# A transformer layer with shared keys and values: two accumulators for the row sums of P, ten P slots, a layer norm split between VectorE and GpSimd, and a new set of planner constants

## The chip, the cores and the metric

The kernel runs on one core of one Trainium2 chip. The core has five engines that run their own instruction streams: TensorE (PE in the profile; its weight loads are listed apart as PEld), VectorE (DVE), ScalarE (ACT), GpSimd (POOL) and SyncE (SP), which here only issues DMAs. The engines wait for one another with semaphores. Data lies in HBM, in the on-chip memory SBUF (128 partitions), and in PSUM, where TensorE writes its results. The metric is the time of one execution on the device in microseconds. Of several executions the median counts.

## What is computed

One layer with 2048 tokens of width 1024: attention with 32 heads of width 32, which all share one key and one value head, then a gated feed-forward of width 3584. All inputs are bf16.

```python
h  = x + attention(layernorm(x)) @ wo
h2 = h + (sigmoid(g) * u) @ w_down      # g = layernorm(h) @ w_gate, u = layernorm(h) @ w_up

# attention, for each of 32 heads
scores = q @ k.T * 32 ** -0.5           # k and v are the same for all heads
p = softmax(scores)
o = p @ v
```

The layer norm subtracts the mean and divides by sqrt(variance + eps).

## The kernel before

**One list for each engine.** The kernel doesn't write its instructions in program order. A planner (class `Plan`) keeps a list for each engine and a model clock. The main loop walks along TensorE's time: it asks which piece of work is ready, appends it to TensorE's list, and the work of the other engines that depends on it goes into heaps, from which `step` takes the one that can start first (of those, the lowest `prio`, which is the most urgent). Every operation carries two costs: `occ`, how long its engine is taken, and `lat`, until its result can be used. Times in the model are ns. At the end the lists are emitted, with semaphore waits where one engine needs another's result. So a changed constant in the dictionary `TUNE` changes the order of instructions on every engine, though not what each computes.

**Halves.** The 16 token tiles of 128 tokens are worked on one after another, and each in two halves of 16 heads: `hf` runs from 0 to 31, `c = hf // 2` is the tile. A half has 16 rounds, one for each key tile `kt`. A round is called S: four matmuls with 32 rows each, on the four row groups of TensorE at once, which write scores of 128 keys by 2048 (head, token) columns into four PSUM banks. Two exponentials on ScalarE (L696), 1024 columns each, write them as bf16 into a **P slot** (`Pr`, 4 KB a partition). PSUM has three pairs of banks for this (`S_ps`), and two banks (`F_ps`) for everything else. The first two halves are interleaved, and four more areas of SBUF serve as slots (`extra`) until their real users come.

**Sums and PV.** The softmax needs the sum of P over all keys. VectorE adds the slots of a half into one accumulator, `acc` (L671): slot 0 plus slot 1, then each further slot, 15 additions. After the last one, TensorE sums over the partitions with 32 small matmuls on `acc` (class SUM). VectorE takes the reciprocal (L737), and two DMAs (L739 and L740) spread it over the partitions. Since there is one accumulator, the first addition of half `hf` waits for SUM of `hf - 1`; if that isn't planned yet, additions are kept in `late_adds` and made up by `flush_adds`. Half 0 is in `RAW`: its sums come from matmuls with a matrix of ones instead. PV multiplies P by V in parts of some rounds (`parts_of`: two parts of eight from half 2 on), in column mode: four matmuls on four column groups. A slot is free when its PV matmuls and its addition are done. A PV part may be chosen only when all its additions are planned, and when `in_row` says so: TensorE is in row mode (just after S), or, with `col_ok`, in column mode, or no more than a given number of slots is free (`pv_few` for PV, `sum_few` for SUM).

**After a tile's two halves**: VectorE multiplies by the reciprocal (`OT`, L754), TensorE multiplies by wo (class OP), VectorE adds x, and the second layer norm follows (`stats` with `ph` 1): statistics on VectorE (L344 to L355), then on GpSimd variance plus eps (L367), power one half (L370) and power minus one (L373), then the normalization on VectorE (L866, tile `hn`) and a transposing DMA to `hnT`. The first layer norm (`ph` 0) runs at the start over x; its first two tiles already use one GpSimd power between two VectorE operations (L359 to L365).

**Feed-forward.** Class GU makes gate and up products in pieces of 512 of the 3584 columns, seven groups of two pieces; ScalarE takes a tanh (L978), VectorE multiplies (L999 or L985). Usually `hnT` is the stationary operand, the result has tokens on partitions, and a transposing DMA (L1008) turns it. For the first `ws0` and the last `ws1` tiles the weights are stationary (`held_w`), which needs no transpose and takes four times as many matmuls of a quarter of the columns. Class D makes the down product in four quarters. Gate and up weights are streamed from HBM for every tile (`load_next`), two units at a time, into eight units of a ring; after the last S, the P slots become such units too.

**Order.** TensorE takes S as soon as its inputs are known and ScalarE has less than 700 ns of work queued; otherwise it goes on with the group in hand, or picks a new one from the classes in the order of `PRIOS`. `start_of` keeps VectorE's additions (`prio` 6) out of a window `hold` around the expected end of TensorE's group, so that VectorE is free to empty its bank. `evac` gives copies out of PSUM to ScalarE or VectorE, whichever is free first, with a bias (`eb` for x, K and V, `eq` for Q) against ScalarE.

Of the kernel before, what the change touches and what calls it, by code (L numbers as in the profile page):

```python
# [15 lines left out]
SEM = 75.0  # L16


TUNE = dict(warm=70, late=400, ws0=1, ws1=2, parts0=3, parts1=4, lord=2, h_ord=0, ho=3, ho2=0, pvl1=0, pvl2=1,
            col_ok=1, pace0=310, swait=400, parts=2, raw=1, rl=0, nd=4, pc=16, rate=315, pace=280, xd=4, qf=1,  # L20
            dall=0, wo_late=1, nkn=2, few=1, rmin=900, hmin=1, h0=0, h1=600, hf=1.35, run=700, sum_few=2,
            pv_few=4, d_off=1, d_a=-1, d_b=-1, eb=150, eq=1000)


class Op:
# [16 lines left out]
class Plan:  # L42
# [53 lines left out]
    def start_of(self, o):  # L96

        s = max(self.free[o.eng], o.ready)
        if o.eng == "dve" and o.prio >= 6 and s < self.hold[1] and s + o.occ > self.hold[0]:
            return self.hold[1]  # L100
        return s

    def step(self, limit):
# [21 lines left out]
        if o.nbytes:  # L125
            if o.pace:
                self.pace_free = s + o.nbytes / TUNE["pace0" if self.fast(s) else "pace"]
            k = o.key.rstrip("0123456789_")
            go = max(s + 1720.0, self.dma_free)
            w = self.SLOW.get(k, 1.0) if k != "ha" else 2.5 if o.nbytes < 200000 else 1.3  # L130
            self.dma_free = go + o.nbytes * w / TUNE["rate"]
            o.end = self.dma_free + 700.0 + self.LATE.get(k, 0.0) + TUNE["late"]
        else:
# [24 lines left out]
def t_dve(n, rate=0.96, fix=158.0):  # L158
    return dict(occ=n / rate + fix - 90.0, lat=n / rate + fix + SEM)
# [5 lines left out]
def bass_sequential_preLN__grouped_kv_mqa__glu_gated_glu__prompt_kernel(  # L165
# [24 lines left out]
    NSLAB = 4  # L190
    SW = 512
    NGR = NFT // 4
    NP = 11
    xf = A_x[0]
    of = out[0]

    with ExitStack() as es:
        def EC(cm):
            return es.enter_context(cm)

        def SB(name, shape, dt=BF16):
            return EC(nc.sbuf_tensor(name, [P] + shape, dt))
# [2 lines left out]
        zone = SB("zone", [NFT * D])  # L205
        ring_t = SB("ring", [NSLAB * DT * SW])
        Pr = SB("Pr", [NP, 2048])
        acc = SB("acc", [2048])
        QTb = SB("QTb", [2, NG, 256])
        wo_sb = SB("wo_sb", [NG, D])  # L210
        kT4 = SB("kT4", [S])
# [98 lines left out]

        for c in ["xxqxxqxxxxxxqxxxxq", "qxqxxqxqxxxxxxxxxx", "xqxqxqqxxxxxxxxxxx", "xqxqxqxqxxxxxxxxxx", "xxqxqxqxqxxxxxxxxx"][TUNE["lord"]]:
            if c == "x":
# [19 lines left out]
        def stats(ph, tiles, srcs, deps, prio, after=((), ())):  # L332
            t0, k = tiles[0], len(tiles)

            def slow(n, wait):

                n += wait if ph and t0 < NT - 1 else 0
                return dict(occ=n, lat=n + 100)

            ag = []  # L340
            for t, src, dp in zip(tiles, srcs, deps):
                s = n_st[0] % 8
                n_st[0] += 1
                a = pl.op("dve", lambda s=s, src=src: DVE.bn_stats(st[:, s, 0, :], src[:, 0:512]), dp, prio=prio,  # L344
                          occ=600, lat=756, order=[st_user.get(s)] + list(after[0]))
                b = pl.op("dve", lambda s=s, src=src: DVE.bn_stats(st[:, s, 1, :], src[:, 512:1024]), dp, prio=prio,  # L346
                          occ=600, lat=756, order=[st_user.get(s)] + list(after[1]))
                c = pl.op("dve", lambda s=s, t=t: DVE.bn_aggr(mv[:, ph, t, :], st[:, s, :, :]), [a, b], prio=prio - 1,
                          occ=110, lat=284)
                st_user[s] = c  # L350
                ag.append(c)
            tk = slice(t0, t0 + k)
            d = pl.op("dve", lambda: DVE.tensor_copy(out=mvb[:, ph, tk, :], in_=mv[:, ph, tk, :]), ag, prio=prio - 1,  # L353
                      occ=90, lat=250)
            e = pl.op("dve", lambda: DVE.tensor_copy(out=mvr[:, ph, tk, :], in_=mvb[:, ph, tk, :]), [d], prio=prio - 1,  # L355
                      occ=90, lat=250)
            if not ph and t0 < 2:

                f = pl.op("dve", lambda: DVE.tensor_scalar(  # L359
                    out=zb[:, ph, tk], in0=mvb[:, ph, tk, 1], scalar1=LN_EPS_BF16, scalar2=None, op0=ALU.add),  # L360
                    [d], prio=prio - 1, occ=90, lat=250)
                g = pl.op("pool", lambda: POOL.tensor_tensor(
                    out=dsb[:, ph, tk], in0=zb[:, ph, tk], in1=half[:, 0:k], op=ALU.pow), [f, c0], prio=0,
                    **slow(460 + 180 * k, 0))
                h = pl.op("dve", lambda: DVE.reciprocal(rstd[:, ph, tk], dsb[:, ph, tk]), [g], prio=prio - 1, occ=90, lat=250)  # L365
                return e, h
            f = pl.op("pool", lambda: POOL.tensor_scalar(  # L367
                out=zb[:, ph, tk], in0=mvb[:, ph, tk, 1], scalar1=LN_EPS_BF16, scalar2=None, op0=ALU.add),
                [d], prio=prio - 1, **slow(330, 920))
            g = pl.op("pool", lambda: POOL.tensor_tensor(  # L370
                out=dsb[:, ph, tk], in0=zb[:, ph, tk], in1=half[:, 0:k], op=ALU.pow), [f, c0], prio=prio - 1,
                **slow(460 + 180 * k, 900))
            h = pl.op("pool", lambda: POOL.tensor_tensor(  # L373
                out=rstd[:, ph, tk], in0=dsb[:, ph, tk], in1=negone[:, 0:k], op=ALU.pow), [g, c1], prio=prio - 1,
                **slow(400 + 180 * k, 0))
            return e, h
# [5 lines left out]
        def center(t):  # L382
            if t >= TUNE["pc"]:
                xcent[t] = pl.op("pool", lambda t=t: POOL.tensor_scalar(
# [30 lines left out]
        for tiles in ([0], [1], [2, 3], [4, 5], [6, 7], [8, 9], [10, 11], [12, 13], [14, 15]):  # L415
            after = ((), ())
            if tiles[0] in (1, 2):

                p = tiles[0] - 1
# [218 lines left out]
        sum_last = {}  # L638
# [14 lines left out]
        RAW = tuple(range(TUNE["raw"])) + ((NH - 1,) if TUNE["rl"] else ())  # L653
        rs_b = h_sb[:, 2, :].bitcast(F32)

        def make_add(hf, kt):

            pred = hf - 1
            if pred not in RAW and pred not in sum_last:
                late_adds[hf].append(kt)  # L660
                return
            a = acc[:, :]
            slot = slot_of[(hf, kt)]
            dp = [exp_of[(hf, kt, i)] for i in range(2)]
            if kt == 1:
                in0 = slot_of[(hf, 0)]
                dp += [exp_of[(hf, 0, i)] for i in range(2)] + [sum_last.get(pred)]
            else:
                in0 = a
                dp.append(add_op[(hf, kt - 1)])  # L670
            add_op[(hf, kt)] = pl.op("dve", lambda: DVE.tensor_tensor(out=a, in0=in0, in1=slot, op=ALU.add), dp, prio=6,  # L671
                                     **t_dve(2048, 1.92))

        def flush_adds(hf):
            for kt in late_adds.pop(hf, []):
                make_add(hf, kt)
# [42 lines left out]
        rd_ld = {}  # L719
# [4 lines left out]
            return v_done[0] >= NV or pl.pe_mode == "row" or len(free_slots) <= few or TUNE["col_ok"] and pl.pe_mode == "col"  # L724

        def mk_SUM(hf):
            a = acc[:, :]

            def atoms(b):
                return [(mm(F_ps[DH * j:DH * (j + 1), b, 0:64], sel[:, bb, :], a[:, j * 512 + bb * 64:j * 512 + (bb + 1) * 64],  # L730
                            bb == 0, bb == 7, tile_position=(0, DH * j)), 64, "col" if j == 3 else "col-", [])
                        for bb in range(8) for j in range(4)]

            def after(b, last):
                sum_last[hf] = last
                flush_adds(hf + 1)
                rc = pl.op("dve", lambda: DVE.reciprocal(r_sb[:, :], F_ps[:, b, 0:64]),  # L737
                           [last, rd_ld.get(hf - 1)], prio=0, occ=64 * 8 / 0.96 + 20, lat=64 * 8 / 0.96 + 90 + SEM)
                rd_ld[hf] = dma(lambda: SP.dma_start(r_dram, r_sb[0:P:4, :]), "rd", 8192, [rc] + (rb_ld[hf - 1] if hf - 1 not in RAW else []), prio=0)  # L739
                rb_ld[hf] = [dma(lambda j=j: SP.dma_start(  # L740
                    rb[DH * j:DH * (j + 1), :], bass.AP(r_dram.tensor, r_dram.offset + 512 * j, [[0, DH], [1, 512]])),
                    "rb", 65536, [rd_ld[hf], ot_ev.get(hf - 1), ot_ev.get(0)], prio=0) for j in range(4)]
                finish(hf)
                return [rc]
            return Group("SUM", atoms, lambda: [add_op.get((hf, NT - 1)), c_sel], after, lambda: in_row(TUNE["sum_few"]))
# [341 lines left out]
        while True:  # L1087
# [15 lines left out]
            if v < NV:  # L1103
                run = max(pl.free["act"], t) + sum(o.occ for o in pl.heap["act"])
# [30 lines left out]
            if cur is not None:  # L1135
                at = cur[1][cur_i]
                if known(at[3], t):
                    mode = at[2]
                    o = pe_op(at[0], at[1], "col" if mode == "col-" else mode, at[3] + (cur[2] if cur_i == 0 else []),
                              mode != "col-")  # L1140
# [152 lines left out]
```

## Time and profile before

| What | Value |
|---|---|
| median of 9 executions | 1102.61 us (1099.27 to 1103.95) |
| the profiled execution, its own time | 1100.76 us |
| its span, first to last instruction | 1099.0 us |
| TensorE matmul busy | 1078.4 us (98%), 10686 matmuls |
| ScalarE busy | 1003.5 us (91%) |
| VectorE busy | 834.4 us (76%) |
| GpSimd busy | 65.3 us (6%) |
| exponentials (L696) | 1024 in all, last one ends at 1012.0 us |
| additions into `acc` (L671) | 465, 1.16 to 1.22 us each |
| GpSimd power operations in the second layer norm (L370, L373) | 1.37 and 1.38 us each in 200 to 1000 us |
| granted TensorE clock | 1.00 throughout |
| HBM traffic | 203.82 MB read, 8.12 MB written, 193 GB/s |

Engine times are the union of an engine's instructions. Matmuls, exponentials and additions are pipelined, so the duration of one is longer than the distance from its start to the next; where it is said how often something can be done, the distance between starts is the measure. A matmul group in the profile is told by its tiles: `S_ps<-QTb,kT` is S, `F_ps<-Pr,Vt` is PV, `F_ps<-acc,sel` is SUM, `F_ps<-wo_sb,OT` is OP, `F_ps<-ring,hnT` is GU, with `hnT,ring` or `hnT,Pr` when the weights are stationary, and `F_ps<-zone,hact` is D.

### The profile page before, as it was taken

What the parts mean: (1) busy time and instruction counts of PE and PEld (TensorE: products, weight loads), DVE (VectorE), ACT (ScalarE), POOL (GpSimd) and SP (SyncE); (2) the same over time, 40 slices, a digit from 0 to 9 for tenths busy, and PEclk for the clock granted to TensorE, in tenths of its full rate; (3) what the DMA queues carried; (4) which work ended last, traced back from release to release, by engine and by line L of the source; (5) the groups of instructions that cost most, each with busy time, mean ns of one, the idle gap of its engine ahead of it and who ended that gap; (6) DMA issues with size and microseconds to landing.
All of it is one profiled execution on the core that took longest, in us unless ns stands there. A gap on an engine that the chain in (4) does not pass through costs nothing.

```text
span 1099.0 us, 25839 instructions
## 1 busy us (share of the span) xinstructions
PE 1078.4 (98%) x10686; PEld 542.6 (49%) x10686; DVE 834.4 (76%) x1055; ACT 1003.5 (91%) x1151; POOL 65.3 (6%) x93
## 2 busy tenths in 40 slices
PE   8899999999999999999999999999999999999999
PEld 6433366444444444444444444444444444436898
DVE  8979887778978687878868686888878686887411
ACT  4999999999999999999999999999999999998110
POOL 3300001010100101010000101010000101010000
DMA  8794389967859595876859496876959596786991
GB/s 247 112 310 125 107 258 317 276 181 211 256 164 270 128 275 155 246 201 198 268 154 261 129 275 162 237 219 189 279 134 259 134 257 175 219 224 182 308 315 62
DMA packets 292804, 232.91 MB, mean 212 GB/s; under 512 B 95824, under 2 KB 279120, under 8 KB 292688
## 3 DMA queue, kind: packets, MB, share of 16 engines
q1 hardware_dynamic: 292688, 231.27, 74.6%
q8 instruction: 84, 1.38, 0.5%
q14 instruction: 32, 0.26, 0.1%
HBM read 203.82 MB, written 8.12 MB: 193 GB/s over the span
## 4 chain that ended last, share of the span: by engine, by line
ACT 44%; PE 35%; issue 7%; DVE 7%; DMA 5%; SPq 2%; POOL 0%; DVEq 0%
ACT Pr L696 41%; PE F_ps L440 30%; PE S_ps L440 5%; DVE acc L671 3%; DMA rb<-r_scratch 2%; ACT tnh L978 2%; DMA r_scratch<-r_sb 1%; SPq L740 1%; DMA ring<-in_A_x_dram 1%; DVE st L346 1%; DMA hnT<-hn 1%; DVE st L344 1%; DMA zone<-ring 0%; SPq L298 0%; DVE h_sb L860 0%
## 5 line engine op out<-in xcount | busy, mean ns | idle before, releaser
L696 ACT ACTIVATE Pr<-S_ps 128x1024 bf16<-128x1024 f32 x1008 | 948.3, 1102 | 5.5 <-PE S_ps L440 5.4
L671 DVE TENSOR_TENSOR acc<-acc,Pr 128x2048 bf16<-128x2048 bf16 x429 | 523.0, 1219 | 13.7 <-ACT Pr L696 0.2
L440 PE MATMUL F_ps<-ring,hnT 128*128 128x512 bf16 x1456 | 359.0, 381 | 0.0
L440 PE MATMUL F_ps<-zone,hact 128*128 128x256 bf16 x1792 | 224.5, 273 | 0.0
L440 PE MATMUL S_ps<-QTb,kT 32*128 32x512 bf16 x2048 | 202.1, 384 | 8.2 <-ACT Pr L696 4.6
L440 PEld LDWEIGHTS F_ps<-ring,hnT 128*128 128x128 bf16 x1456 | 124.4, 98 | 165.4 <-issue 46.9
L440 PEld LDWEIGHTS F_ps<-zone,hact 128*128 128x128 bf16 x1792 | 165.1, 98 | 49.6 <-issue 24.0
L440 PEld LDWEIGHTS S_ps<-QTb,kT 32*128 32x128 bf16 x2048 | 51.6, 91 | 189.4 <-ACT Pr L696 146.8
L440 PE MATMUL F_ps<-Pr,Vt 128*32 128x512 bf16 x2016 | 138.0, 382 | 0.5 <-DVE h_sb L860 0.2
L978 ACT ACTIVATE tnh<-F_ps 128x512 f32<-128x512 f32 x112 | 75.0, 670 | 60.7 <-PE F_ps L440 60.7
L1046 DVE SCALAR_TENSOR_TENSOR h_sb<-F_ps,h_sb 128x256 bf16<-128x256 f32 x64 | 26.7, 417 | 97.6 <-PE F_ps L440 97.5
L999 DVE SCALAR_TENSOR_TENSOR act_s<-tnh,F_ps 128x512 bf16<-128x512 f32 x91 | 62.0, 681 | 31.2 <-PE F_ps L440 31.0
L440 PE MATMUL F_ps<-zone 128*128 128x512 bf16 (+3 forms) x584 | 75.7, 274 | 4.9 <-DMA zone<-in_A_wq_dram 1.3
L440 PEld LDWEIGHTS F_ps<-Pr,Vt 128*32 128x32 bf16 x2016 | 46.3, 95 | 62.8 <-issue 29.0
L440 PE MATMUL F_ps<-wo_sb,OT 128*128 128x512 bf16 x256 | 63.4, 380 | 1.2 <-DVE act_s L999 0.6
L367 POOL TENSOR_SCALAR zb<-mvb 128x1 bf16<-128x1 bf16 (+1 forms) x23 | 5.1, 222 | 967.1 <-DVE mvb L353 967.1
L440 PE MATMUL F_ps<-hnT,ring 128*128 128x128 bf16 x912 | 59.7, 219 | 0.5 <-DMA ring<-in_B_w_gate_dram 0.2
L440 PEld LDWEIGHTS F_ps<-zone 128*128 128x128 bf16 x584 | 39.0, 97 | 34.6 <-issue 9.9
L440 PEld LDWEIGHTS F_ps<-hnT,ring 128*128 128x128 bf16 x912 | 52.2, 98 | 7.4 <-issue 5.9
L737 DVE RECIPROCAL r_sb<-F_ps 128x64 f32<-128x64 f32 x31 | 17.3, 557 | 47.2 <-PE F_ps L440 47.1
L985 DVE SCALAR_TENSOR_TENSOR hact<-tnh,F_ps 128x512 bf16<-128x512 f32 x21 | 14.4, 685 | 33.2 <-PE F_ps L440 33.2
L440 PEld LDWEIGHTS F_ps<-wo_sb,OT 128*128 128x128 bf16 x256 | 22.2, 97 | 31.2 <-issue 6.9
(75 smaller groups left out, 430.1 us busy)
## 6 DMA issues: line engine op xcount, KB each, us to landing
ring<-in_B_w_gate_dram SPq DMA_DIRECT2D x308, 256.0 KB, 4.1
ring<-in_B_w_up_dram SPq DMA_DIRECT2D x304, 256.0 KB, 4.1
rb<-r_scratch SPq DMA_DIRECT2D x124, 64.0 KB, 2.8
zone<-in_B_w_down_dram SPq DMA_DIRECT2D x14, 512.0 KB, 5.1
Pr<-in_B_w_up_dram SPq DMA_DIRECT2D x24, 256.0 KB, 5.2
Pr<-in_B_w_gate_dram SPq DMA_DIRECT2D x20, 256.0 KB, 5.0
ring<-in_A_x_dram SPq DMA_DIRECT2D x16, 256.0 KB, 6.7
h_sb<-in_A_x_dram SPq DMA_DIRECT2D x16, 256.0 KB, 3.0
```

The source lines that it names most:

```text
L344: a = pl.op("dve", lambda s=s, src=src: DVE.bn_stats(st[:, s, 0, :], src[:, 0:512]), dp, prio=prio, occ=600, lat=756, order=[st_user.get(s ...
L346: b = pl.op("dve", lambda s=s, src=src: DVE.bn_stats(st[:, s, 1, :], src[:, 512:1024]), dp, prio=prio, occ=600, lat=756, order=[st_user.ge ...
L367: f = pl.op("pool", lambda: POOL.tensor_scalar(out=zb[:, ph, tk], in0=mvb[:, ph, tk, 1], scalar1=LN_EPS_BF16, scalar2=None, op0=ALU.add), ...
L440: return lambda: PE.matmul(o, lhsT=l, rhs=r, start=start, stop=stop, **kw)
L671: add_op[(hf, kt)] = pl.op("dve", lambda: DVE.tensor_tensor(out=a, in0=in0, in1=slot, op=ALU.add), dp, prio=6, **t_dve(2048, 1.92))
L696: exps[u] = pl.op("act", lambda i=i, pb=pb: ACT.activation(out=slot[:, i * 1024:(i + 1) * 1024].rearrange("p (a b) -> p a b", a=2), in_=S_ ...
L737: rc = pl.op("dve", lambda: DVE.reciprocal(r_sb[:, :], F_ps[:, b, 0:64]), [last, rd_ld.get(hf - 1)], prio=0, occ=64 * 8 / 0.96 + 20, lat=6 ...
L740: rb_ld[hf] = [dma(lambda j=j: SP.dma_start(rb[DH * j:DH * (j + 1), :], bass.AP(r_dram.tensor, r_dram.offset + 512 * j, [[0, DH], [1, 512]])),
L978: box["a"] = pl.op("act", lambda: ACT.activation(out=tnh[:, :], in_=F_ps[:, b, :], func=ACTF.Tanh, scale=0.5), [last, box.get("e")], prio= ...
L985: e = pl.op("dve", lambda: DVE.scalar_tensor_tensor(out=ho, in0=tnh[:, :].rearrange("p (f b) -> p f b", b=P), scalar=1.0, in1=F_ps[:, b, : ...
L999: e = pl.op("dve", lambda: DVE.scalar_tensor_tensor(out=so, in0=tnh[:, :], scalar=1.0, in1=F_ps[:, b, :], op0=ALU.add, op1=ALU.mult), [las ...
L1046: e = pl.op("dve", lambda: DVE.scalar_tensor_tensor(out=h_sb[:, t % NHB, sl], in0=F_ps[:, b, 0:DW], scalar=0.5, in1=h_sb[:, t % NHB, sl], ...
```

## The change

- `acc` has two rows; half `hf` uses row `hf % 2`, and its first addition waits for SUM of `hf - 2` instead of `hf - 1`. To make room, P has ten slots instead of eleven.
- In the second layer norm (`ln_v`) variance plus eps and the reciprocal are VectorE operations, as in the first two tiles of the first one; GpSimd does one power.
- `start_of`: a VectorE addition isn't started if an operation with more urgent priority becomes ready within the next 500 ns (`look`).
- The planner's costs of an addition and of the reciprocal are given as numbers.
- Of the constants in `TUNE`, two are new (`look`, `ln_v`) and sixteen have other values.

```diff
--- before.py
+++ after.py
@@ -16,10 +16,10 @@
 SEM = 75.0
 
 
-TUNE = dict(warm=70, late=400, ws0=1, ws1=2, parts0=3, parts1=4, lord=2, h_ord=0, ho=3, ho2=0, pvl1=0, pvl2=1,
-            col_ok=1, pace0=310, swait=400, parts=2, raw=1, rl=0, nd=4, pc=16, rate=315, pace=280, xd=4, qf=1,
-            dall=0, wo_late=1, nkn=2, few=1, rmin=900, hmin=1, h0=0, h1=600, hf=1.35, run=700, sum_few=2,
-            pv_few=4, d_off=1, d_a=-1, d_b=-1, eb=150, eq=1000)
+TUNE = dict(look=500, ln_v=1, warm=70, late=400, ws0=1, ws1=1, parts0=3, parts1=3, lord=2, h_ord=2, ho=3,
+            ho2=0, pvl1=0, pvl2=0, col_ok=0, pace0=310, swait=400, parts=2, raw=1, rl=0, nd=4, pc=16, rate=315,
+            pace=250, xd=4, qf=1, dall=1, wo_late=1, nkn=3, few=0, rmin=900, hmin=1, h0=100, h1=250, hf=1.35,
+            run=700, sum_few=0, pv_few=3, d_off=1, d_a=-1, d_b=0, eb=700, eq=400)
 
 
 class Op:
@@ -97,7 +97,12 @@
 
         s = max(self.free[o.eng], o.ready)
         if o.eng == "dve" and o.prio >= 6 and s < self.hold[1] and s + o.occ > self.hold[0]:
-            return self.hold[1]
+            s = self.hold[1]
+        if o.eng == "dve" and o.prio >= 6:
+
+            for p in self.heap["dve"]:
+                if p.prio < 6 and s < p.ready < s + TUNE["look"]:
+                    return p.ready
         return s
 
     def step(self, limit):
@@ -190,7 +195,7 @@
     NSLAB = 4
     SW = 512
     NGR = NFT // 4
-    NP = 11
+    NP = 10
     xf = A_x[0]
     of = out[0]
 
@@ -205,7 +210,7 @@
         zone = SB("zone", [NFT * D])
         ring_t = SB("ring", [NSLAB * DT * SW])
         Pr = SB("Pr", [NP, 2048])
-        acc = SB("acc", [2048])
+        acc = SB("acc", [2, 2048])
         QTb = SB("QTb", [2, NG, 256])
         wo_sb = SB("wo_sb", [NG, D])
         kT4 = SB("kT4", [S])
@@ -354,14 +359,14 @@
                       occ=90, lat=250)
             e = pl.op("dve", lambda: DVE.tensor_copy(out=mvr[:, ph, tk, :], in_=mvb[:, ph, tk, :]), [d], prio=prio - 1,
                       occ=90, lat=250)
-            if not ph and t0 < 2:
+            if ph and TUNE["ln_v"] or not ph and t0 < 2:
 
                 f = pl.op("dve", lambda: DVE.tensor_scalar(
                     out=zb[:, ph, tk], in0=mvb[:, ph, tk, 1], scalar1=LN_EPS_BF16, scalar2=None, op0=ALU.add),
                     [d], prio=prio - 1, occ=90, lat=250)
                 g = pl.op("pool", lambda: POOL.tensor_tensor(
                     out=dsb[:, ph, tk], in0=zb[:, ph, tk], in1=half[:, 0:k], op=ALU.pow), [f, c0], prio=0,
-                    **slow(460 + 180 * k, 0))
+                    **slow(460 + 180 * k, 900))
                 h = pl.op("dve", lambda: DVE.reciprocal(rstd[:, ph, tk], dsb[:, ph, tk]), [g], prio=prio - 1, occ=90, lat=250)
                 return e, h
             f = pl.op("pool", lambda: POOL.tensor_scalar(
@@ -655,11 +660,11 @@
 
         def make_add(hf, kt):
 
-            pred = hf - 1
-            if pred not in RAW and pred not in sum_last:
+            pred = hf - 2
+            if pred >= 0 and pred not in RAW and pred not in sum_last:
                 late_adds[hf].append(kt)
                 return
-            a = acc[:, :]
+            a = acc[:, hf % 2, :]
             slot = slot_of[(hf, kt)]
             dp = [exp_of[(hf, kt, i)] for i in range(2)]
             if kt == 1:
@@ -669,7 +674,7 @@
                 in0 = a
                 dp.append(add_op[(hf, kt - 1)])
             add_op[(hf, kt)] = pl.op("dve", lambda: DVE.tensor_tensor(out=a, in0=in0, in1=slot, op=ALU.add), dp, prio=6,
-                                     **t_dve(2048, 1.92))
+                                     occ=1135, lat=1255)
 
         def flush_adds(hf):
             for kt in late_adds.pop(hf, []):
@@ -724,7 +729,7 @@
             return v_done[0] >= NV or pl.pe_mode == "row" or len(free_slots) <= few or TUNE["col_ok"] and pl.pe_mode == "col"
 
         def mk_SUM(hf):
-            a = acc[:, :]
+            a = acc[:, hf % 2, :]
 
             def atoms(b):
                 return [(mm(F_ps[DH * j:DH * (j + 1), b, 0:64], sel[:, bb, :], a[:, j * 512 + bb * 64:j * 512 + (bb + 1) * 64],
@@ -733,9 +738,9 @@
 
             def after(b, last):
                 sum_last[hf] = last
-                flush_adds(hf + 1)
+                flush_adds(hf + 2)
                 rc = pl.op("dve", lambda: DVE.reciprocal(r_sb[:, :], F_ps[:, b, 0:64]),
-                           [last, rd_ld.get(hf - 1)], prio=0, occ=64 * 8 / 0.96 + 20, lat=64 * 8 / 0.96 + 90 + SEM)
+                           [last, rd_ld.get(hf - 1)], prio=0, occ=480, lat=560 + SEM)
                 rd_ld[hf] = dma(lambda: SP.dma_start(r_dram, r_sb[0:P:4, :]), "rd", 8192, [rc] + (rb_ld[hf - 1] if hf - 1 not in RAW else []), prio=0)
                 rb_ld[hf] = [dma(lambda j=j: SP.dma_start(
                     rb[DH * j:DH * (j + 1), :], bass.AP(r_dram.tensor, r_dram.offset + 512 * j, [[0, DH], [1, 512]])),
```

## The prediction

> **What bounds the kernel now.** I read the span in slices first, then the waits, one tile of tokens in the middle of the run, and the end. The windows (start:end in us, then PE, PEld, DVE, ACT and POOL busy with counts) show two engines full at once:
>
> ```profile
> 0.00:27.50 27.50, 22.06 (x322) 19.05 (x323) 22.81 (x64) 13.04 (x20) 9.30 (x32) 1.00 0.85 247
> 27.50:55.00 27.50, 23.24 (x297) 13.51 (x296) 26.88 (x69) 27.32 (x35) 10.34 (x14) 1.00 0.71 112
> ...
> 440.00:467.50 27.50, 27.40 (x240) 12.75 (x242) 23.28 (x26) 27.50 (x33) 0.00 (x0) 1.00 0.84 249
> 467.50:495.00 27.50, 27.50 (x227) 12.30 (x222) 20.29 (x26) 27.49 (x33) 2.97 (x3) 1.00 0.71 197
> ```
>
> PE lacks work only early: 27.5 minus its busy time, summed over the first seven slices, is 15.4 us, of which 9.7 lie before 55 us; later slices show 27.40 or 27.50. ACT is full from the second slice on. VectorE (23.28, 20.29) has air, GpSimd is all but idle.
>
> The chain of waits repeats itself every 62.29 us (one token tile, two halves):
>
> ```profile
> 258.76 2.07 PE F_ps L440 x18
> ...
> 321.05 2.07 PE F_ps L440 x18
> ...
> 383.34 2.07 PE F_ps L440 x18
> ```
>
> What PE does in such a period is counted in the groups of the window 436.0 to 498.3: 112 gate/up matmuls, 112 down matmuls, 128 S (one above by the window's edge), 128 PV, 16 OP, 64 SUM. The prices are in the timeline:
>
> ```profile
> 961.60 1.47 PE L440 MATMUL F_ps<-ring,hnT 128*128 128x512 bf16 x6
> 963.00 0.40 PE L440 MATMUL S_ps<-QTb,kT 32*128 32x512 bf16 x4
> 963.33 2.12 PE L440 MATMUL F_ps<-ring,hnT 128*128 128x512 bf16 x9
> 965.38 0.40 PE L440 MATMUL S_ps<-QTb,kT 32*128 32x512 bf16 x4
> ```
>
> Starts are 1.40 us apart around 6 matmuls and 2.05 around 9: 0.65/3 = 0.217 us for one of 512 columns, which leaves 0.10 for going from full-array work to S. S takes 0.33 where a round of four that run together should take 0.217, so coming back costs 0.11. Down matmuls (256 columns) go at 0.109 (28 in 3.06 us late in the run). A tile is then 112 x 0.217 + 112 x 0.109 + 32 x 0.217 (S) + 32 x 0.217 (PV) + 16 x 0.217 + 0.5 (SUM) = 54.4 us. The remaining 7.9 of 62.29 are some 72 changes between full-array, row and column work at 0.11. **PE is packed**, a seventh of it with changes. The 146.8 us in which weight loads for S wait for ACT are no air of the same size: the matmul row is busy meanwhile.
>
> ACT has little more room: nine exponentials start in 8.19 us (449.09 to 457.28), 0.910 each, and a tanh takes 0.48 to 0.55; 64 and 7 of them make 61.6 to 62.1. The last exponential ends at 1012.0; what follows is PE alone, 83.86 us busy out of 84.3.
>
> **Two accumulators, ten slots.** With one accumulator the first addition of a half waits for SUM of the half before, and VectorE stands still:
>
> ```profile
> 520.87 0.69 DVE L999 SCALAR_TENSOR_TENSOR act_s<-tnh,F_ps 128x512 bf16<-128x512 f32 x1 [1.10 <-PE F_ps L440]
> 524.09 0.56 DVE L737 RECIPROCAL r_sb<-F_ps 128x64 f32<-128x64 f32 x1 [2.54 <-PE F_ps L440]
> 524.57 1.16 DVE L671 TENSOR_TENSOR acc<-Pr 128x2048 bf16<-128x2048 bf16 x1
> ```
>
> The S round of 511.78 already belongs to the new half, yet its first addition starts at 524.57. Afterwards it can start some 9 us earlier. The 15 additions stay, 1.22 us long, 30 a tile = 34 us at 1.14 each, so the arithmetic is worth 0; the PE packing hides it. What changes on PE is where SUM and PV start. In the tile shown, the PV part at 511.45 enters from full-array work with 4 matmuls and is cut by two S rounds: three stretches where two would do, one change too many. With additions planned earlier and the threshold lowered (`pv_few` 4 to 3) I take one change a tile as saved, 0.11 x 15 = 1.7 us. Bounds: all some 7 changes beyond two per S round, 7 x 0.11 x 15 = 11.6 us saved; or, as `col_ok=0` forbids SUM to start in the shadow of a PV part, two changes more a tile, 3.3 us lost. I take the near end because the two SUM pieces of this tile (523.59 and 558.92) already follow an S directly.
>
> The lost slot: from 511.78 to 529.35 there are ten S rounds of the half, and PV of its first eight starts at 529.68. Ten slots just hold that; the eleventh is the cover for a slip. Expected cost 0; without cover a slip keeps S, and so ACT, waiting (priced below). In the tail the P slots take weights in pairs with 8 pieces of the ring: 19 pieces make 9 pairs, 18 make 9 too, so 0.
>
> **Layer norm.** For each of 16 tiles two GpSimd instructions, 0.22 (zb) and 1.38 us (second pow), become two on VectorE like L359 and L365, 0.148 and 0.150. The chain from variance to `hn` shortens by 1.60 - 0.30 = 1.3 us; VectorE gains 0.3 us of work a tile. The chain ends in a transpose whose next reader is gate/up work of a later stretch, and PE always has other work (0.35 us idle in the tail before hnT), so 0; without the cover it is a gain of 1.3 us once, at the last tile. The sharper point is the pow that stays: it takes 1.37 us inside the run and 0.79 at the head, where no additions run. [...]
>
> **Order on VectorE.** The new `look` keeps an addition from starting when urgent work is due within 500 ns. The idle time it makes is at most 0.5 us before about 30 urgent instructions a tile, 15 us in the worst case, where VectorE has 13 free (busy 23.28 + 20.29 in the 55 us of the two slices above, so 49 of 62.29). It would free banks sooner, but PE waits for VectorE in only a few places (4.7 us for `acc` in 187 to 934, by weight loads). I take 0, bounds -4.7 and, through late slots, the rival below.
>
> **Held weights for one tile fewer** (`ws1` 2 to 1). Tile 14's 14 pieces go from 32 matmuls of 128 columns to 8 of 512:
>
> ```profile
> 1013.21 5.53 PE L440 MATMUL F_ps<-hnT,ring 128*128 128x128 bf16 x96
> 1018.58 2.35 PE L440 MATMUL F_ps<-zone,hact 128*128 128x256 bf16 x20
> ```
>
> 96 take 5.37 us, so a piece is 1.79 against 8 x 0.217 = 1.73: 0.06 x 14 = 0.8 us saved. It adds four transposing DMAs on SP's queue, each with 1.57 us of issue and 3.5 to landing; queued behind them are weight loads and the output. Tile 14's down product starts at 1052.02, 5.7 us after its last gate/up matmul, so it is covered; uncovered it costs 3.5.
>
> **Early part** (`h_ord`, `eb`, `eq`, `parts1`, `nkn`, `dall`). `eb` 700 pushes kT, Vt and x evacuations from ACT to VectorE; `eq` 400 pulls Q evacuations to ACT. Between 27.5 and 192.5 us PE idles 10.0 us in sum. I take a quarter of it as recovered, 2.5; bounds: all 10.0, or, if the 24 Q evacuations of 512 columns move to ACT at a tanh's 0.48, 11.5 us of delay of the exponentials.
>
> **Pacing and prefetch.** `pace` 280 to 250: one tile loads about 40 pieces of 256 KB, 10.5 MB, 42 us at 250 GB/s out of 62. Hidden; 0.
>
> **Sum:** 1.7 + 0.8 + 2.5 = 5.0 us. The profiled execution took 1100.76 us with a span of 1099.0; its span would be 1094. It lies 1.85 below the median of 1102.61, so on the median's scale I predict 1097.5. About 0.2%, 2.2 us, is what a measurement can tell from no change.
>
> **Rivals.**
>
> *PE sheds enough changes to reach ACT's floor.* Period 61.6 instead of 62.29, 0.7 x 14 = 10 us, with 2.5 and 0.8 from above 13: 1089.5. For it: seven changes a tile are avoidable. Against: each is worth 0.11 and S rounds must stay single, since ACT frees S banks one after another. 14%.
>
> *Nothing that binds is touched.* PE work and ACT work are the same, the idle times of VectorE and GpSimd were free: 1102.6. For it: every moved instruction is on an engine with air. Against: the early idle time of PE surely changes somehow. 14%.
>
> *Ten slots are too few* (ends slower). The place is the eleventh S round of each half (531.30 in the tile shown), which needs a slot from a PV part that began only one round before. If `look` or a late PV holds that back by more than the 0.7 us that ACT has over in a period, each further 0.1 us counts. A third of a round, 0.3 us, in 30 halves is 9 us: 1112 with nothing gained. For it: `few=0` and the waiting additions cut the same cover. Against: PV itself need not wait for SUM any more. 20%.
>
> *Q evacuations on ACT* (ends slower). In the stage to 150 us ACT idles 0.2 us a slice and PE has no feed-forward work yet; about 7 of the 11.5 us stay: 1109. 10%.
>
> **How the numbers follow.** Forecast 42%, own range 1090 to 1100.4. Faster: 42 + 14 = 56%; same 14%; slower 20 + 10 = 30%. The range goes from below ACT's floor case, 1086, to the ten-slot case, 1112.
>
> **What would show it.** Right: the period stays within 0.3 us of 62.29, SUM starts within some 5 us of its half's last exponential, VectorE's waits for PE at L737 (41.8 us in 187 to 934) mostly go, PE idles less before 192 us, and the tail stays one packed PE stretch of about 83 us. Wrong: S waits with ACT idle inside the halves, a longer period, or more ACT copies before 150 us with a later last exponential than 1012.0.

## The result and the profile after

The changed kernel takes 1097.51 us, the median of 11 executions (1095.49 to 1101.24); the kernel before takes 1101.64 (34 executions). The ratio is 0.9962, with a 95% interval of 0.9953 to 0.9972: about 4.2 us faster. The profiled execution of the changed kernel took 1098.94 us with a span of 1097.1, so it is a rather slow one of its kind, while that of before (1100.76) was a quick one; between these two the last matmul ends only 1.8 us earlier (1094.46 instead of 1096.29). What follows reads this pair, so it can account for 1.8 us; the rest of the 4.2 lies in how the executions of each kernel spread.

The middle of the run is nearly what it was. The chain of waits in a window of the changed kernel (start, length, what):

```profile
532.51 1.62 PE F_ps L445 x28
...
594.74 1.62 PE F_ps L445 x28
...
656.98 1.62 PE F_ps L445 x28
```

The period is 62.23 and 62.24 us where it was 62.29. VectorE, on the other hand, looks quite different. Its timeline around the end of a half:

```profile
518.67 0.69 DVE L801 TENSOR_TENSOR oun<-F_ps,oun 128x512 f32<-128x512 f32 x1 [1.38 <-PE F_ps L445]
519.37 0.56 DVE L742 RECIPROCAL r_sb<-F_ps 128x64 f32<-128x64 f32 x1
519.85 1.16 DVE L676 TENSOR_TENSOR acc<-Pr 128x2048 bf16<-128x2048 bf16 x1
```

and the list of its waits from 187 to 934 us (total, times, longest):

```profile
DVE acc L676 <- ACT Pr L701: 49.4, 100, 1.1
...
DVE r_sb L742 <- PE F_ps L445: 8.8, 11, 0.8
...
DVE h_sb L1051 <- PE F_ps L445: 2.1, 6, 0.8
```

Before, two of these lines stood at the top of VectorE's waits in the same stretch (L737 is now L742, L1046 is L1051):

```profile
DVE h_sb L1046 <- PE F_ps L440: 64.7, 12, 5.4
DVE r_sb L737 <- PE F_ps L440: 41.8, 24, 2.5
```

Now additions wait for the exponential they need, 49.4 us in 100 short pieces, and the copies of PV's result (`oun`) wait 40.4 us for TensorE where they waited 0.3: the sums keep pace with P. SUM starts 3.4 or 7.3 us after the last exponential of its half from 300 us on, where it was 11.1 or 15.4. The look ahead isn't what makes the short pieces: without it (e6) they are 105.3 us in 173, while with one accumulator (e2) only 4.5 us in 9 are left.

TensorE has less idle time early. The windows of the first 192.5 us that changed most (columns as before):

```profile
27.50:55.00 27.50, 26.35 (x311) 14.68 (x307) 26.75 (x70) 27.50 (x37) 9.18 (x15) 1.00 0.70 145
55.00:82.50 27.50, 27.37 (x257) 10.06 (x253) 22.68 (x27) 27.50 (x31) 0.00 (x0) 1.00 1.00 319
...
137.50:165.00 27.50, 24.62 (x373) 16.83 (x371) 22.76 (x24) 26.63 (x32) 0.00 (x0) 0.94 0.96 308
```

In the first two, PE was busy 23.24 and 25.62 us before. The third got worse (26.68 before), and the clock column says 0.94; more on this below. The second and the third as they were:

```profile
55.00:82.50 27.50, 25.62 (x291) 9.78 (x289) 21.22 (x26) 27.50 (x32) 0.00 (x0) 1.00 0.97 309
...
137.50:165.00 27.50, 26.68 (x401) 17.35 (x398) 23.85 (x26) 27.48 (x33) 0.00 (x0) 1.00 0.82 258
```

Idle time before 192.5 us is 11.4 us in sum instead of 15.4. Part of that is lost again in the middle; the first line is the kernel before, the second the changed one:

```profile
192.50:934.00 741.50, 740.37 (x6665) 333.30 (x6664) 581.06 (x677) 741.41 (x847) 35.67 (x36) 1.00 0.76 211
192.50:934.00 741.50, 738.40 (x6659) 332.39 (x6656) 598.31 (x704) 740.59 (x845) 17.40 (x12) 1.00 0.76 209
```

TensorE stands still for 3.1 us there instead of 1.1, most of it in front of gate and up matmuls (2.3 us): after SUM, for instance, they wait 0.17 us for VectorE to empty a bank (519.46).

The tail is still one packed stretch, 80.4 us from the last exponential (1014.1) to the last matmul, with 0.8 us idle:

```profile
1034.17 1.89 PE L445 MATMUL F_ps<-ring,hnT 128*128 128x512 bf16 x8 [0.17 <-issue]
1035.89 1.89 PE L445 MATMUL F_ps<-Pr,hnT 128*128 128x512 bf16 x8
1037.62 3.22 PE L445 MATMUL F_ps<-zone,hact 128*128 128x256 bf16 x28
1040.68 3.62 PE L445 MATMUL F_ps<-Pr,hnT 128*128 128x512 bf16 x16
1044.13 3.74 PE L445 MATMUL F_ps<-hnT,Pr 128*128 128x128 bf16 x64
```

Tile 14's pieces are 8 matmuls of 512 columns now, 1.72 us from start to start; tile 15's, from 1044.13 on, are still 32 of 128. The last exponential ends 2.1 us *later* than before (1014.1, 1012.0) and the kernel ends earlier. ScalarE is full in the middle in both, and what TensorE still has to do after the last exponential, 80.4 us instead of 84.3, sets the end.

**A ledger.** TensorE's time is work, mode changes between full-array, row and column matmuls at some 0.11 us (read from the starts in the trace of before), idle time, and what a lower clock adds. Counted in the two traces up to the last matmul: idle time 17.9 and 15.5 us (end minus busy), so -2.5; mode changes 1135 and 1134, so -0.1; tile 14's pieces -0.8; a stretch of 3.4 us at half clock, +1.7. The sum is -1.7, the measured difference -1.8. It doesn't close this well everywhere (see e7 and e8).

### The profile page after: what moved, and what is told of

The parts are those of the page before. It is cut to its first block, busy times and chain, and to the rows that moved or that the text cites. A ratio compares the mean times of both kernels' runs of the same rounds, so it can differ in the third digit from the quotient of the medians.

```text
span 1097.1 us, 25358 instructions
## 1 busy us (share of the span) xinstructions
PE 1079.0 (98%) x10350; PEld 528.9 (48%) x10350; DVE 851.0 (78%) x1087; ACT 1003.5 (91%) x1151; POOL 39.6 (4%) x61
## 4 chain that ended last, share of the span: by engine, by line
PE 69%; ACT 21%; DMA 4%; issue 3%; DVE 2%; SPq 1%; POOL 0%; DVEq 0%
PE F_ps L445 58%; ACT Pr L701 18%; PE S_ps L445 11%; DMA rb<-r_scratch 1%; DMA ring<-in_B_w_up_dram 1%; ACT tnh L983 1%; DVE acc L676 1%; DMA ring<-in_A_x_dram 1%; SPq L745 0%; DMA r_scratch<-r_sb 0%; SPq L303 0%; SPq L312 0%; ACT h_sb L701 0%; ACT hact L701 0%; ACT QTb L701 0%
## 5 line engine op out<-in xcount | busy, mean ns | idle before, releaser
L445 PE MATMUL F_ps<-ring,hnT 128*128 128x512 bf16 x1536 | 382.6, 380 | 2.6 <-issue 1.9
L445 PEld LDWEIGHTS F_ps<-ring,hnT 128*128 128x128 bf16 x1536 | 131.3, 97 | 176.8 <-issue 59.6
L1004 DVE SCALAR_TENSOR_TENSOR act_s<-tnh,F_ps 128x512 bf16<-128x512 f32 x98 | 67.0, 683 | 25.4 <-PE F_ps L445 25.2
L367 POOL TENSOR_TENSOR dsb<-zb,cst 128x1 bf16<-128x1 bf16 x18 | 23.0, 1278 | 968.4 <-DVE zb L364 968.4
L1051 DVE SCALAR_TENSOR_TENSOR h_sb<-F_ps,h_sb 128x256 bf16<-128x256 f32 x64 | 26.8, 419 | 28.4 <-PE F_ps L445 28.3
L801 DVE TENSOR_TENSOR oun<-F_ps,oun 128x512 f32<-128x512 f32 x34 | 23.4, 688 | 25.9 <-PE F_ps L445 25.9
L445 PE MATMUL F_ps<-hnT,ring 128*128 128x128 bf16 x608 | 40.0, 223 | 1.1 <-issue 0.7
L445 PEld LDWEIGHTS F_ps<-hnT,ring 128*128 128x128 bf16 x608 | 35.6, 100 | 6.9 <-issue 6.1
L797 DVE COPY oun<-F_ps 128x512 f32<-128x512 f32 x32 | 22.1, 690 | 20.5 <-PE F_ps L445 20.4
L676 DVE TENSOR_TENSOR acc<-Pr 128x2048 bf16<-128x2048 bf16 x31 | 37.0, 1193 | 0.1
```

The costliest lines, as they stand in the source:

```text
L367: g = pl.op("pool", lambda: POOL.tensor_tensor(out=dsb[:, ph, tk], in0=zb[:, ph, tk], in1=half[:, 0:k], op=ALU.pow), [f, c0], prio=0, **sl ...
L445: return lambda: PE.matmul(o, lhsT=l, rhs=r, start=start, stop=stop, **kw)
L797: oun_ev[(hf, 0)] = pl.op("dve", lambda: DVE.tensor_copy(out=o, in_=F_ps[:, b, :]), [last, ot_ev.get(hf - 2)], prio=0, **t_dve(512))
L801: oun_ev[(hf, part)] = pl.op("dve", lambda: DVE.tensor_tensor(out=o, in0=F_ps[:, b, :], in1=o, op=ALU.add), [last, oun_ev[(hf, part - 1)]] ...
L1004: e = pl.op("dve", lambda: DVE.scalar_tensor_tensor(out=so, in0=tnh[:, :], scalar=1.0, in1=F_ps[:, b, :], op0=ALU.add, op1=ALU.mult), [las ...
L1051: e = pl.op("dve", lambda: DVE.scalar_tensor_tensor(out=h_sb[:, t % NHB, sl], in0=F_ps[:, b, 0:DW], scalar=0.5, in1=h_sb[:, t % NHB, sl], ...
```

## Experiments

Two readings were open. One is that of the prediction: each part of the change has a price of its own, and the prices add up. The other is the theory of the order: whatever is edited, the planner deals all of TensorE's list anew; the time follows idle time and mode changes in that list, and the parts named in the change have hardly a price by themselves. Its forecasts are read from the planner's lists. The planner ends TensorE's list at 1090.5 us on its own clock for the kernel before and at 1087.2 for the changed one (the last matmuls ended at 1096.3 and 1094.5). Ratios below are to the kernel before, with 95% intervals; a distance to the changed kernel is the difference of its ratio to 0.9962, times 1101.6 us.

### Held weights back (e1)

```diff
-ws1=1
+ws1=2
```

> The changed kernel with weights held for the last two tiles again (ws1=2). Theory of the terms: tile 14's 14 pieces cost 1.79 instead of 1.73 us each, so 0.8 us more than the changed kernel, nothing else. Theory of the order (any new constant makes the planner deal the whole order anew, and the time follows where TensorE is left without work in the new order): the planner's own clock ends its TensorE list 1.9 us later, 0.8 from the pieces and 1.1 from idle time elsewhere in the list, so 1.9 us more.

Measured: 1098.29 us, ratio 0.9968 (0.9954 to 0.9983), 0.7 us more than the changed kernel. The term's 0.8 fits; 1.9 lies inside the interval too, so this run doesn't tell the two apart.

### One accumulator (e2), ten slots in the kernel before (e3), two accumulators in the kernel before (e4)

```diff
# e2, against the changed kernel
-            pred = hf - 2
-            if pred >= 0 and pred not in RAW and pred not in sum_last:
+            pred = hf - 1
+            if pred not in RAW and pred not in sum_last:
...
-            a = acc[:, hf % 2, :]
+            a = acc[:, 0, :]
...
-                flush_adds(hf + 2)
+                flush_adds(hf + 1)
# e3, against the kernel before; e4 has this, and the two rows of acc
-    NP = 11
+    NP = 10
```

> The changed kernel with one accumulator, ten slots, and all else as changed. If the accumulators are the whole gain: 4.1 us more, the time of before. By the prediction's term (one mode change a tile): 1.7 us more. Theory of the order: the planner's list has 31 more mode changes (3.4 us) and 1.8 us more idle time on TensorE, so 5.2 us more.

> The kernel before with ten P slots instead of eleven, one accumulator, nothing else changed. If the eleventh slot is unneeded cover: no change. By the ten-slot rival of the prediction (0.3 us of waiting in 30 halves): 9 us more than before. Theory of the order: 26 more mode changes (2.8 us) and 6.5 us more idle time on TensorE, 9.3 us more, with the exponentials still running back to back in the middle.

> The kernel before with two accumulators and ten slots, all constants as before. If the accumulators are the whole gain: 4.1 us less than before. If they only pay for the lost slot: no change against before, and 9 us less than the same kernel with ten slots and one accumulator. Theory of the order: the old constants were chosen for another order, 24 more mode changes and 7.2 us more idle time on TensorE, 9.8 us more than before.

Measured: e2 1100.92 us, ratio 0.9989 (0.9973 to 1.0004), 3.0 us more than the changed kernel. e3 1108.71 us, 1.0060 (1.0040 to 1.0081), 6.6 us more than before. e4 1109.28 us, 1.0065 (1.0042 to 1.0088), 7.2 us more than before. So the lost slot has a price in the old order, below the 9 us of the ten-slot rival, and the second accumulator doesn't pay for it there. The price doesn't arise as the rival had it, with ScalarE kept waiting: in e3 ScalarE is busy 740.7 of the 741.5 us from 192.5 to 934, and its last exponential ends at 1011.6 (1012.0 before); but TensorE then still has 92.0 us to go instead of 84.3. With the new constants and two accumulators no run has eleven slots, so the slot's price there is not shown; the second accumulator is worth about 3 us there. Neither is a price of the part: it depends on the order. e2 also shows how little VectorE's idle time says; its waits from 187 to 934 us are back near where they were before:

```profile
DVE h_sb L1051 <- PE F_ps L445: 62.3, 14, 5.4
DVE r_sb L742 <- PE F_ps L445: 37.1, 22, 3.4
```

These are 88 us of VectorE's time more than in the changed kernel, and the kernel is 3 us slower.

### The layer norm on GpSimd again (e5)

```diff
-ln_v=1
+ln_v=0
```

> The changed kernel with the second layer norm's three operations on GpSimd again (ln_v=0). The lists of TensorE and ScalarE are the same, instruction by instruction, as in the changed kernel. By the prediction's term: the chain to hn is 1.3 us longer and covered by TensorE's work, 0 us, at most 1.3 at the last tile. If the layer norm's chain is on the path: 1.3 us in each of 16 tiles, up to 20 us more. Theory of the order: same order on TensorE, so 0 us.

Measured: 1097.59 us, ratio 0.9966 (0.9953 to 0.9979), 0.4 us more than the changed kernel and within the intervals: no effect that can be told. This is the cleanest of the runs, since TensorE's and ScalarE's lists stay as they are.

### No look ahead (e6)

```diff
-look=500
+look=0
```

> The changed kernel without the look ahead for urgent VectorE work (look=0). By the prediction's term: 0 to 4.7 us more. If the waiting additions cost anything (the slower rival): faster than the changed kernel. Theory of the order: 16 more mode changes (1.7 us) and 8.8 us more idle time on TensorE, so 10.5 us more, slower than the kernel before too.

Measured: 1105.74 us, ratio 1.0042 (1.0028 to 1.0056), 8.8 us more than the changed kernel: the theory of the order, by far. Part of the idle time is in the tail, which the timeline shows (in brackets the idle time before, and what ended it):

```profile
1014.98 1.89 PE L445 MATMUL F_ps<-ring,hnT 128*128 128x512 bf16 x8 [0.59 <-DVE oun L801]
...
1026.54 1.89 PE L445 MATMUL F_ps<-wo_sb,OT 128*128 128x512 bf16 x8 [1.20 <-DVE OT L759]
...
1049.47 0.81 PE L445 MATMUL F_ps<-ring,hnT 128*128 128x512 bf16 x3 [1.55 <-DMA ring<-in_B_w_up_dram]
```

The ledger holds here as well: in the profiled executions 21.6 us idle (6.1 more than the changed kernel), 1150 changes (16 more, 1.7 us), no half-clock stretch (-1.7) make 6.1; the last matmul ends 6.4 us later. What remains for TensorE after the last exponential is 89.5 us here, against 80.4.

### Code without constants (e7), constants without code (e8)

> The changed kernel's code (two accumulators, ten slots, one GpSimd power, look ahead) with the sixteen constants as before. If the parts of the code bring the gain: about the changed kernel's time, 4 us less than before. Theory of the order: 19 more mode changes and 8.9 us more idle time than in the changed kernel, 11.8 us more than it and 8 us more than before.

> The kernel before (one accumulator, eleven slots, three GpSimd operations, no look ahead) with the sixteen new constants. If the constants bring the gain: about the changed kernel's time, 4 us less than before. Theory of the order: constants and code only fit each other; 21 more mode changes and 4.3 us more idle time than before, 5.7 us more than before.

Measured: e7 1104.93 us, ratio 1.0033 (1.0022 to 1.0043), 3.6 us more than before. e8 1102.54 us, 1.0009 (0.9997 to 1.0020), 1.0 us more. Neither half of the change brings anything alone. The theory of the order has the sign of e7 and sizes that are too large (7.8 against 11.8 us more than the changed kernel; 1.0, not clear of no change, against 5.7). The ledger doesn't close for this pair of profiled executions: for e7 it gives 8.7 us more than the changed kernel (idle time 4.1, 19 changes 2.1, held weights 0.8, a stretch of 6.83 us at half clock instead of 3.41 1.7), and the last matmul ends 5.6 us later; for e8 it gives 2.9 more than before (idle time 1.4, 21 changes 2.3, tile 14's pieces -0.8), and 1.8 were measured. What it misses is not shown.

### Small matmuls in the idle time (e9)

```diff
+            if v < NV and 100000.0 < t < 180000.0:
...
+                if bs and idle % 3 == 0:
...
+                    pl.op("pe", mm(F_ps[:, bs[0], 0:P], ident[:, :], ident[:, :], True, True), list(bank_rel[bs[0]]), occ=0.0, lat=250.0)
```

> The kernel before with two accumulators, ten slots and the old constants (8.0 us slower than before in its own run), in the same order, plus 46 small matmuls on the identity into an idle bank, put where TensorE's list has no work between 148 and 166 us. In the profile of that kernel TensorE stood still for most of 148 to 151 us, and its granted clock was 0.50 from 151.5 to 158.4 us. Theory of the clock (idle time of TensorE costs twice: itself, and a stretch at half clock afterwards): no stretch at 0.50 before the end, and up to 3.4 us (half of 6.8) less than without the small matmuls, so about 1106. Rival, idle time costs only itself: the same 1109 or, for the added work, a little more.

Measured: 1108.63 us, ratio 1.0052 (1.0032 to 1.0071), against 1.0065 for e4: 1.4 us less, inside both intervals. The clock is another matter. The windows of e4,

```profile
150.00:151.00 1.00, 0.00 (x0) 0.00 (x0) 0.99 (x2) 1.00 (x3) 0.00 (x0) 1.00 0.93 301
...
155.00:156.00 1.00, 1.00 (x16) 0.19 (x8) 0.41 (x1) 0.55 (x1) 0.00 (x0) 0.50 0.88 283
156.00:157.00 1.00, 1.00 (x12) 0.25 (x12) 0.81 (x1) 0.04 (x1) 0.00 (x0) 0.50 0.90 286
```

and of e9:

```profile
150.00:151.00 1.00, 0.58 (x23) 0.28 (x6) 0.99 (x2) 1.00 (x3) 0.00 (x0) 1.00 1.08 344
...
155.00:156.00 1.00, 1.00 (x24) 0.39 (x20) 0.39 (x2) 1.00 (x2) 0.00 (x0) 1.00 1.02 298
156.00:157.00 1.00, 1.00 (x19) 0.49 (x11) 1.00 (x2) 1.00 (x2) 0.00 (x0) 1.00 1.04 265
```

The clock column (third from the right) still reads 0.50 five us after the empty microsecond of e4, and even ScalarE starves (0.55, 0.04); with the small matmuls it stays at 1.00 and ScalarE is full. All seven executions of e4 have a mean clock below 1 (0.997 or 0.998), all six of e9 have 1.000. So the stretch at half clock went with the idle time; that it costs 3.4 us here is not shown: 1.4, with an interval that takes in zero.

### The early constants (e10) and another order (e11)

```diff
# e10, against the changed kernel
-parts1=3, h_ord=2, dall=1, nkn=3, eb=700, eq=400
+parts1=4, h_ord=0, dall=0, nkn=2, eb=150, eq=1000
# e11, against the changed kernel
-look=500, late=400, ws1=1, parts0=3, parts1=3, ho2=0, pvl2=0, col_ok=0, pace0=310, swait=400
-pace=250, dall=1, few=0, hmin=1, run=700, pv_few=3, d_off=1, d_a=-1, d_b=0, eb=700, eq=400
+look=700, late=200, ws1=2, parts0=4, parts1=4, ho2=3, pvl2=1, col_ok=1, pace0=290, swait=200
+pace=265, dall=0, few=2, hmin=0, run=1000, pv_few=1, d_off=0, d_a=1, d_b=1, eb=0, eq=700
```

> The changed kernel with the six constants of the early part as before (h_ord, eb, eq, parts1, nkn, dall). By the prediction's term of the early part: 2.5 us more than the changed kernel, all of it as idle time of TensorE before 192.5 us. If the early part is the whole gain: 4.1 us more. Theory of the order: 24 more mode changes (2.6 us) and 5.6 us more idle time, spread over the run, 8.2 us more.

> The changed kernel with other constants in TUNE, chosen for nothing but the end of TensorE's list on the planner's own clock, with an eye to no long idle stretch before 180 us (weights held for the last two tiles again, DMAs taken as 0.2 us quicker, exponentials queued up to 1000 ns ahead). Theory of the order: 21 more mode changes (2.3 us), 5.9 us less idle time and 0.8 us more for the held weights, 2.8 us less than the changed kernel, and up to 1.7 us less in executions where the changed kernel has its 3.4 us at half clock: about 1094. Rival, the named parts of the change carry the gain and the constants only have to be tolerable: 1098 or more.

Measured: e10 1102.91 us, ratio 1.0004 (0.9990 to 1.0018), 4.6 us more than the changed kernel: the whole gain is gone, between the 2.5 of the term and the 8.2 of the list, and nearest to the 4.1 of the second forecast. From 27.5 to 192.5 us its trace has 10.0 us of idle time, as before the change, against 5.8 in the changed kernel; that is an upper bound, since 110 of its 10350 matmuls are missing from the trace. e11 1096.44 us, 0.9943 (0.9924 to 0.9962), 2.1 us less than the changed kernel, where 2.8 were expected from the list; its interval ends where the changed kernel's ratio lies, and its six executions have a clock of 1.000. It is faster than before beyond doubt, than the changed kernel probably. Part of that small distance can be the clock: the executions of the changed kernel at a clock of 1.000 have a median of 1097.2. e11 keeps the code of the change, with a longer `look`, and five of the sixteen constants (`h_ord`, `nkn`, `h0`, `h1`, `sum_few`), and holds weights for two tiles. So it shows that the other constants of the change aren't needed for the gain; what the code alone is worth it doesn't show, and e7 says that with the old constants it is worth nothing.

The planner's new costs of an addition, the reciprocal and the power were not undone by themselves, nor were the constants that only e7, e8 and e11 touch.

### Mode changes added (e12)

```diff
+                    if v == NV and cur[0].cls == "D" and cur_i in (4, 10, 16, 22) and not held and known(bank_rel[1 - cur_b], t):
...
+                        if cur_i in (10, 22):
+                            pl.op("pe", mm(F_ps[0:DH, ob, 0:64], ones[:, :], ident[:, 0:64], True, True, tile_position=(0, 0)),
+                                  list(bank_rel[ob]), occ=0.0, lat=250.0)
+                        else:
+                            pl.op("pe", mm(F_ps[:, ob, 0:64], ident[:, :], ident[:, 0:64], True, True), list(bank_rel[ob]), occ=0.0, lat=250.0)
```

> The changed kernel, same order, with 30 small matmuls of 64 columns set into the down product's quarters after the last S, where TensorE has no idle time: 20 on one column group (two mode changes each) and 10 on the full array (none). They write a bank that nobody uses at that moment. If a change costs 0.11 us, as read from the distances in the trace of before: 0.25 to 0.28 us for each of the 20, 0.03 to 0.06 for each of the 10, in sum 5.3 to 6.2 us more than the changed kernel. If changes cost nothing of their own (the 0.11 is something else about S): 0.9 to 1.8 us more.

Measured: 1101.66 us, ratio 0.9998 (0.9985 to 1.0011), 4.0 us more than the changed kernel. The timeline prices each one:

```profile
1087.12 0.19 PE L445 MATMUL F_ps<-ident 128*128 128x64 bf16 x1
1087.14 0.82 PE L445 MATMUL F_ps<-zone,hact 128*128 128x256 bf16 x6
1087.89 0.20 PE L445 MATMUL F_ps<-ident,ones 128*32 128x64 bf16 x1
1088.03 1.92 PE L445 MATMUL F_ps<-zone,hact 128*128 128x256 bf16 x16
```

From a down matmul past a small full-array one to the next takes 0.137 us in each of the 10 cases, and past one on a column group 0.338 in the mean of 20; without either it is 0.109. So the small matmul itself costs 0.028 and two mode changes 0.201: **0.10 us a change** between full array and one column group, measured by itself. 20 x 0.229 + 10 x 0.028 make 4.9 us, and 4.0 came out at the end, less than the 5.3 to 6.2 forecast and more than the 0.9 to 1.8 of changes that cost nothing.

## Why the prediction was right, point by point

**What bounds the kernel** held. TensorE is packed, a change of mode costs 0.10 (e12; taken as 0.10 to 0.11), and the ledger of work, changes, idle time and clock closes to 0.1 us for the change and 0.3 for e6, though only to 3 for e7 and 1 for e8. (7.9 of 62.29 us of changes are an eighth, not the seventh that the prediction writes.) Of its signs, the period, VectorE's waits for SUM and the packed tail (80.4 us, some 83 forecast) came; SUM comes within 5 us of the last exponential in every second half only.

**Two accumulators: one change a tile, 1.7 us** failed as a sum, though the mechanism exists. In 249 to 934 us, eleven periods, the traces hold 781 and 771 changes, almost one a tile fewer, as taken. But from 62 to 125 us there are ten more (70 and 80), and the total is 1135 and 1134. The forced entry of PV that was to vanish is still there (four PV matmuls at 516.26, then S). The term was 0.1, not 1.7, in the ledger. Within the new order the second accumulator saves more: e2's trace, without it, holds 1164 changes, 30 more than the changed kernel's, which at 0.10 each is the 3 us that it is slower.

**Ten slots: 0** fits the new order, where nothing shows that S waits for a slot, and would be wrong in the old one: e3 costs 6.6 us. There too ScalarE doesn't wait, so the rival had a price but not its way: TensorE is left with more to do at the end.

**The layer norm: 0** is shown by e5 (0.4 us, within the intervals). The pow that stays takes 1.45 us instead of 1.37, and from 200 to 1000 us nobody waits for it. In both kernels one addition is running when this pow starts, and the pow ends some 0.4 us after that addition, which ends 1.05 us after the pow's start here and 0.96 before. Where VectorE runs nothing beside it, as at 107.50 and 1036.44 us, the pow takes 0.55 us.

**`look`: 0, bounds 0 to -4.7** was mis-sized: without it the changed kernel is 8.8 us slower (e6), beyond the bound. The prediction looked only for waits that it could remove from the old order, not for the order that the planner would find with it.

**Held weights: 0.8** fits (e1 0.7, which doesn't exclude 1.9). **The early part: 2.5** was taken too small, and what it left out went the other way: idle time between 27.5 and 192.5 us fell from 10.0 to 5.8, 4.2 and not 2.5, but 1.5 us of idle time came back after 192.5 us, and 1.7 went to the half-clock stretch in the profiled execution. Undoing it costs more than the term, 4.6 us (e10), in a list with 24 more mode changes.

**The rival of the Q evacuations** didn't come: with `eq` 400 alone the lists of the kernel before come out the same, and in the changed kernel's trace ScalarE takes 8 copies into `hact` instead of 6 but 14 copies out of PSUM in all, as before. Half of the sign named for it did come, a last exponential later than 1012.0 (1014.1), and it didn't cost anything at the end: TensorE had less left to do.

The forecast of 1097.5 thus came out by a sum in which 1.7 too much for mode changes stood against early idle time that was taken too small. That it agrees to 0.01 us is luck twice over: the prediction took 5.0 us from a median of 1102.61 for the kernel before, and the result is 4.2 us below one of 1101.64. What carried it was the bound, not the terms: with TensorE packed and ScalarE full, a new order moves the time mainly by the idle time and the mode changes left.

## What to carry to other kernels

Where a planner or a list scheduler writes the order, an edit is not priced by the instructions that it moves but by the list that comes out; undoing one constant or one part of this change cost up to 9 us, more than twice what the whole change gained. Keep a ledger of the bounding engine (work, mode changes, idle time, clock) and read every version by it, knowing that here it missed up to 3 us; the planner's own end of TensorE's list ordered the runs almost as the chip did (the kernel before and e2 stand the other way round, and e6 and e7), with distances about a fifth too large from end to end (15.9 us from e11 to e4 by the lists, 13.4 measured) and further off for single runs (e8). An engine's idle time that vanishes from the waits, like VectorE's here, is no gain unless the bounding engine gets work sooner for it.

## What was not expected of the hardware

In the changed kernel TensorE's idle time cost twice in one place. TensorE stood still for 1.5 us in all between 143.9 and 146.2 (0.43 and 1.09 us, waiting with S for ScalarE), and the clock then fell:

```profile
144.00:146.00 2.00, 0.74 (x36) 0.40 (x36) 2.00 (x3) 2.00 (x3) 0.00 (x0) 1.00 1.08 371
146.00:148.00 2.00, 1.78 (x18) 1.56 (x19) 1.90 (x4) 2.00 (x4) 0.00 (x0) 0.63 1.12 354
148.00:150.00 2.00, 2.00 (x20) 1.37 (x18) 1.90 (x2) 1.13 (x2) 0.00 (x0) 0.52 1.07 346
```

The stretch at half clock lasted 3.41 us (146.53 to 149.94). In e4 TensorE stood still for 1.80 us between 148 and 151, and the clock read 0.50 from 151.5 to 158.4, 6.8 us; in e3 it stood for 1.61 us between 164 and 166, and the clock read 0.50 from 166.7 to 170.1, 3.4 us (both idle times are upper bounds, since some matmuls are missing from these two traces). As much idle time was not always followed by a fall. The 3.41 us just before the fall in the changed kernel held 1.52 us of it; those from 18.09 us on in the same trace held 1.75, those from 61.75 on in the trace of before 1.62, and there the clock stayed at 1.00. What decides is not shown. The same list can lose its clock or keep it: of 12 executions of the changed kernel 4 show a mean clock below 1.000, and of 83 executions of the kernel before in the rounds of the experiments 15 do.

In the changed kernel the median of the 8 executions at a clock of 1.000 is 1097.2 us and of the 4 others 1098.6, a difference near the 1.7 us that half of 3.41 makes, though four executions are few. The planner's account of idle time doesn't hold this second price.
